# Three buffers instead of two for the filter and second-stage weight tiles of a Fourier transform, paid for out of the software DMA scratch

## The chip, the cores and the metric

The kernel runs on one core of a Trainium2 chip. The metric is the device time of one execution in microseconds (us). Engines are named as in the profile: PE is the matrix engine, PEld its weight loads, DVE the vector engine, ACT the scalar engine, POOL the general engine, SP the engine that here only issues transfers.

## What is computed

The input `x` has 8 batches of 3072 tokens with 256 channels. Three layers follow one another, all in float32:

```
Y   = rfft(x over tokens) * (filt_r + i filt_i);  y = irfft(Y)
k   = relu(xk @ w_k);  v = (k*k) @ w_v;  r = sigmoid(xr @ w_r);  x2 = r * v
h   = max(x2 @ w1, x2 @ w2, x2 @ w3);  out = h @ w_out
```

Here `xk` and `xr` are mixes of `y` with `y` shifted by one token. The hidden widths are 1024 (`w_k`, `w_v`) and 768 (`w1` to `w3`).

## The kernel before

**Precision.** Most products are made of three products of shortened operands: each operand is split into a high part (a copy by ACT) and the remainder (a subtraction by POOL or DVE), in `split` (lines 177 to 179), and `mm3` (line 155) issues the three matmuls. So nearly every matmul needs results of ACT and of POOL or DVE first.

**The transform.** The 3072-point transform of a batch is done in stages, each a matmul, with intermediate arrays `s1` and `s2` in DRAM. Batch 0 has its own code (`fft_first`, lines 423 to 562), before everything else. Batches 1 to 7 are done in `fft(b)` (lines 328 to 421), one batch ahead, in pieces that are threaded between the matmuls of the two dense layers by `drive` (line 108), by weights. Stage A has 16 steps (`a_load`, `a_mm`). Stages B and C have 12 steps for two groups of frequencies each:

- `b_load(s)` loads the weights of the step, tile `wbc` (512 KB, 4 KB in each of the 128 partitions; for batch 1 from the input through a software DMA that POOL issues, line 367, with a copy stored to DRAM by ACT, line 369; for later batches from that copy through SP, line 371), the filter, tile `filt` (512 KB, again 4 KB in each partition, line 373), and the data `xb` (line 375), which it splits into `xbh` (ACT) and `xbl` (POOL).
- `b_mm(s)` makes six matmuls with `wbc` (the profile calls the result `pb`), multiplies by the filter in place (DVE, lines 389 to 391, and POOL, line 392), and splits the product into `yh` and `yl` (line 395).
- `c_mm(s)` makes six matmuls with the other half of the same `wbc` tile (result `pc`) and stores the result to `s2`.

The order of the pieces is: `b_load(s)`, `b_mm(s-1)`, then `c_mm(s-2)`. A `wbc` tile is thus held from `b_load(s)` until `c_mm(s)`, two steps later; a `filt` tile from `b_load(s)` until `yl` has been made, one step later.

**Buffers.** Pool `fp` has two buffers for each tag. Tiles of one tag share these buffers:

```
f = fp.tile([NK, 2, 2, C], F32, tag="filt", name="filt")     # line 372; "wst" of piece(), lines 197, 199
w = fp.tile([NK, 4, 2, NK], F32R, tag="wbc", name="wbc")     # line 364; "wvs" 271, "hs" 292, "e1" 473
```

Tag `filt` also serves as the place into which the raw dense weights are loaded (`wst`, up to about 330 us); tag `wbc` also holds the split dense weights on their way to DRAM (`wvs`, `hs`) and one in three of the evacuated results of `fft_first` (`e1`). A transfer into a tile is issued only when the tile that used the buffer before has been read for the last time.

**The dense layers.** Tokens are handled in 64 chunks of 384. `kv` does the first layer for one chunk, `second` the second layer for a pair of chunks with seven products for a 2 by 2 block product. Their weights `w_v` and `w1` to `w3` are streamed anew for every chunk or pair through the pool `ws` (10 buffers, tile `ws`, line 265, up to 8 loads ahead, issued by SP). PE results in the second layer carry the names `pa`, `pb` and `pe` as well: `pb<-x,ws` is a matmul of the dense layer, `pb<-xbh,wbc` one of the transform.

**Order.** Every engine and every issuing queue works in order. Outside `fft_first` that order is laid down when the program is built, from a simulated timeline (`schedule_with_timeline_sim=True`, line 936), in which the order of the code is the priority. SP's order is written out by hand up to line 862.

**Scratch.** [...] POOL issues 17 transfers in all: one of `wa_s` (line 167), four of `wvs` (line 273), 12 of `wbc` (line 367).

Of the kernel before, what the change touches and what calls it, by code (L numbers as in the profile page):

```python
# [9 lines left out]
F32 = mybir.dt.float32  # L10
F32R = mybir.dt.float32r
I32 = mybir.dt.int32
# [11 lines left out]
NK = 2 * N2  # L24
# [70 lines left out]
def as_float(bits):  # L95
    return float(np.uint32(bits).view(np.float32))
# [29 lines left out]
def tile_spectral_moe(ctx: ExitStack, tc, x, filt, ones, wa, wa1, wi, wbc, wb1, wc1, filt1, filt0, mu, w_k, w_v, w_r, w1, w2, w3, w_out, out):  # L126
    nc = tc.nc
    B = x.shape[0]
    P = 128
    C = 256  # L130
# [13 lines left out]
    fp = ctx.enter_context(tc.tile_pool(name="fp", bufs=2))  # L144
# [7 lines left out]
    def mm(o, wgt, rhs, start, stop, more=False):  # L152
        nc.tensor.matmul(o, lhsT=wgt, rhs=rhs, start=start, stop=stop, skip_group_check=more)  # L153
# [23 lines left out]
    def split(hi, lo, src, lo_eng=None):  # L177
        nc.scalar.copy(hi, src)  # L178
        (lo_eng or nc.gpsimd).tensor_tensor(lo, src, hi.bitcast(F32), ALU.subtract)  # L179
# [4 lines left out]
    def piece(src, kt, t0, t1, c0, c1, parts):  # L184

        wide = src.dtype != F32
        if wide:
            src = src.bitcast(I32)
        v = src.rearrange("(t p) n -> p t n", p=P)
        a, c = t1 - t0, c1 - c0  # L190
        st = {}

        def load(stage=None):
            if stage is not None:
                st["t"] = stage.rearrange("p (a n) -> p a n", a=a)
            elif wide:
                st["t"] = fp.tile([P, a, 2 * c], I32, tag="filt", name="wst")
            else:
                st["t"] = fp.tile([P, a, c], F32, tag="filt", name="wst")
            k = 2 if wide else 1  # L200
            nc.sync.dma_start(st["t"], v[:, t0:t1, k * c0 : k * c1])

        def narrow(late=True):
            if not wide:
                st["r"] = st["t"]
                return
            w = st["t"].rearrange("p a (n k) -> p a n k", k=2)
            low, high = w[:, :, :, 0], w[:, :, :, 1]

            e = fp.tile([P, a, c], I32, tag="fo", name="we")  # L210
            ef = e.bitcast(F32)
            nc.scalar.activation(ef, high.bitcast(F32), AF.Abs)
            nc.vector.tensor_scalar(ef, ef, as_float(0x38000000), as_float(0x47EFFFFF), op0=ALU.max, op1=ALU.min)
            nc.vector.tensor_scalar(e, e, 3, 0x3FFFFFFF, op0=ALU.logical_shift_left, op1=ALU.bitwise_and)
            nc.vector.scalar_tensor_tensor(e, high, -0x40000000, e, ALU.bitwise_and, ALU.bitwise_or)
            m = fp.tile([P, a, c], I32, tag="fin", name="wm")
            mf = m.bitcast(F32)
            nc.vector.tensor_scalar(m, e, -0x800000, None, op0=ALU.bitwise_and)
            nc.vector.scalar_tensor_tensor(mf, low.bitcast(U32), 2.0**-52, mf, ALU.mult, ALU.mult)
            cnt[0] += 1  # L220
            r = fp.tile([P, a, c], F32, tag=("flo", "fhi")[cnt[0] % 2], name="wf")
            nc.gpsimd.tensor_tensor(r, ef, mf, ALU.add)
            st["r"] = r

        return load, narrow, lambda late=True: parts(st["r"], late)

    def to_parts(hi, lo, r, late):
        if late:
            nc.scalar.copy(hi, r)
        else:  # L230
            nc.vector.tensor_copy(hi, r)
        nc.gpsimd.tensor_tensor(lo, r, hi.bitcast(F32), ALU.subtract)
# [35 lines left out]

    def wv_job(q):
        def parts(r, late):  # L270
            t = fp.tile([P, 2, 2, C], F32R, tag="wbc", name="wvs")
            to_parts(t[:, :, 0], t[:, :, 1], r, late)
            nc.gpsimd.dma_start(wv_d[q], t.bitcast(F32))

        return piece(w_v, NF, 2 * q, 2 * q + 2, 0, C, parts)

    def wu_job(k):

        fq, j = divmod(k, 3)

        def parts(r, late):


            b11, b12, b21, b22 = (r[:, q, n * P : (n + 1) * P] for q in range(2) for n in range(2))
            sums = [[(0, b11)], [(0, b22), (1, b12), (0, b11)], [(0, b21)], [(0, b12), (1, b11)],
                    [(0, b22), (1, b12)], [(0, b22)], [(0, b12), (1, b11), (1, b22), (0, b21)]]
            for a, e in ((0, 4), (4, 7)):
                q = ps.tile([P, e - a, P], F32, tag="pm", name="ps")
                for n in range(a, e):
                    for at, (sign, of) in enumerate(sums[n]):  # L290
                        mm(q[:, n - a], eye[:, sign], of, n == a and at == 0, at == len(sums[n]) - 1, True)
                t = fp.tile([P, 4, 2, P], F32R, tag="wbc", name="hs")[:, : e - a]
                nc.scalar.copy(t[:, :, 0], q)
                nc.vector.tensor_tensor(t[:, :, 1], q, t[:, :, 0].bitcast(F32), ALU.subtract)
                nc.sync.dma_start(wu_d[k][:, a:e], t.bitcast(F32))

        return piece((w1, w2, w3)[j], 2, 0, 2, 2 * P * fq, 2 * P * (fq + 1), parts)
# [30 lines left out]
    def fft(b):  # L328
# [5 lines left out]
        st = {}  # L334
# [26 lines left out]
            pieces.append((0.65, pa))  # L361

        def b_load(s):
            w = fp.tile([NK, 4, 2, NK], F32R, tag="wbc", name="wbc")
            if b == 1:

                nc.gpsimd.dma_start(w, wbc[:, s])
                wbc_d[s] = dp.tile([NK, 4, 2, NK], F32, tag=f"wbcd{s}", name=f"wbcd{s}", bufs=1)
                nc.scalar.dma_start(wbc_d[s], w.bitcast(F32))
            else:  # L370
                nc.sync.dma_start(w.bitcast(F32), wbc_d[s])
            f = fp.tile([NK, 2, 2, C], F32, tag="filt", name="filt")
            nc.sync.dma_start(f, filt[:, s])
            t = fp.tile([NK, 2, C], F32, tag="fin", name="xb")
            nc.sync.dma_start(t, s1.rearrange("m r g c -> (m r) g c")[:, 2 * s : 2 * s + 2, :])
            hi = fp.tile([NK, 2, C], F32R, tag="fhi", name="xbh")
            lo = fp.tile([NK, 2, C], F32R, tag="flo", name="xbl")
            split(hi, lo, t)
            st["b", s] = w, f, hi, lo
# [27 lines left out]
        for s in range(NBS + 2):  # L407
            def pb(s=s):
                if s < NBS:
                    b_load(s)  # L410
                if 1 <= s <= NBS:
                    b_mm(s - 1)
            def pc(s=s):
                if s >= 2:
                    c_mm(s - 2)
            pieces.append((0.65, pb))
            if s == 0:

                pieces.append((6.0, lambda: None))
            pieces.append((0.65, pc))  # L420
        return pieces

    def fft_first(pp, jobs):
# [7 lines left out]
        p = ps.tile([P, 2, C], F32, tag="pm", name="pz")  # L431
# [7 lines left out]
        for s in range(NM // LX):  # L439
            t = pp.tile([NP, LX, C], F32, tag="big", name="x0", bufs=4)  # L440
# [29 lines left out]

        def evac(i, p, d, q=nc.sync):
            pool, tag = (fp, "wbc") if i % 3 == 2 else (pp, "fo1")
            o = pool.tile(list(p.shape), F32, tag=tag, name="e1", bufs=2 if pool is fp else 4)
            nc.scalar.copy(o, p)
            q.dma_start(d, o)

# [17 lines left out]
        for s in range(NM // 2):  # L494
            p = ps.tile([NQ, 2, C], F32, tag="pm", name="pa")
            mm(p, wa_f, xt[2 * s // LX][:, 2 * s % LX : 2 * s % LX + 2], True, True)
            evac(s, p, s1[2 * s : 2 * s + 2].rearrange("m r g c -> (r g) m c"))
            if s == 1:
                wb_load(0)
            if s == 4:  # L500
                nc.sync.dma_start(f0, filt0)
                f_load(0)
            if s == 6:
                wc_load(0)
                jobs[0][1](False)
                jobs[0][2](False)
# [17 lines left out]
        for s in range(NG // 2 + 2):  # L524
# [9 lines left out]
            if s < NG // 2:  # L534
                p = ps.tile([NK, 2, C], F32, tag="pm", name="pb")
# [3 lines left out]
                f = ft[s]  # L539
# [9 lines left out]
            if s >= 2:  # L549
                f, q = ft[s - 2], qs[s - 2]  # L550
                p = ps.tile([NK, 2, C], F32, tag="pm", name="pc")
                for k in range(2):
                    g = 2 * (s - 2) + k
                    mm(p[:, k], wt[g // LW][1][:, g % LW], f[:, k], True, False)
                    mm(p[:, k], wt[g // LW][2][:, g % LW], q[:, k], False, True)
                evac(s, p, s2.rearrange("m r g c -> (m r) g c")[:, 2 * s - 4 : 2 * s - 2, :], nc.scalar)
# [306 lines left out]
    for _ in range(8):  # L863

        p = ps.tile([P, NT], F32, tag="pm", name="pz")
# [102 lines left out]
```

## Time and profile before

| quantity | value |
|---|---|
| median of three runs | 3239.52 us (3239.22 to 3243.35) |
| profiled execution, first to last instruction (its span) | 3228.3 us |
| what lies around the span, against the median | 11.2 us |
| instructions | 55882 |
| PE busy | 3117.6 us, 97% of the span |
| DVE, ACT, POOL busy | 1774.2, 1918.9, 1865.8 us (55, 59, 58%) |
| bytes moved by transfers | 676 MB, 210 GB/s |

The profile is of one execution, taken by the hardware profiler. For the profiled execution itself nothing but its span is recorded; the 11.2 us is the median less that span. A wait is the time in which an engine sat idle ahead of an instruction, put down to what came last. [...]

### The profile page before, as it was taken

The page shows a single profiled execution, that of the slowest core. Times are in us where ns is not written, and L with a number is a line of the kernel's source. Part 1 is how long each engine was busy: PE and PEld are TensorE (multiplying, and loading weights), DVE is VectorE, ACT ScalarE, POOL GpSimd, SP SyncE. Part 2 cuts the span into 40 slices and gives each one's busy share as a digit, 9 for nine tenths or more (in the row PEclk, how much of TensorE's full clock was granted, in tenths as well). Part 3 has the DMA queues.
Part 4 walks back from the last instruction along what each step waited for, and adds up shares of the span by engine and source line. Part 5 has one row for each costly group of instructions (what it writes and reads, how often), then busy time and mean ns, then how long its engine had stood idle before and what let it go on. Part 6 is the DMA issues. An engine that isn't in the chain of part 4 may idle for free.

```text
span 3228.3 us, 55882 instructions
## 1 busy us (share of the span) xinstructions
PE 3117.6 (97%) x19256; PEld 3039.7 (94%) x19256; DVE 1774.2 (55%) x2882; ACT 1918.9 (59%) x4024; POOL 1865.8 (58%) x1619
## 2 busy tenths in 40 slices
PE   6799899999999999999999999999999999999998
PEld 4799889999999999999999999999999999999998
DVE  4865554556554565456545465445654456555554
ACT  5556556656566566656566556665656666555554
POOL 3545665557555675546756566565655567544443
PEclk8899999999999999999999999999999999999999
DMA  8767786657765676657766577655876657655553
GB/s 283 239 231 220 227 299 202 194 174 259 238 196 187 208 244 201 214 170 234 252 196 186 179 252 246 198 187 166 271 237 189 190 191 242 197 162 163 169 163 123
DMA packets 397783, 676.38 MB, mean 210 GB/s; under 512 B 41920, under 2 KB 153664, under 8 KB 396864
## 3 DMA queue, kind: packets, MB, share of 16 engines
q1 hardware_dynamic: 328336, 585.61, 57.1%
q10 hardware_dynamic: 66752, 78.75, 7.1%
q0 software_dynamic: 2416, 8.46, 0.9%
q8 instruction: 156, 2.56, 0.3%
q14 instruction: 123, 1.01, 0.1%
HBM read 580.51 MB, written 92.14 MB: 208 GB/s over the span
## 4 chain that ended last, share of the span: by engine, by line
PE 79%; DMA 8%; DVE 7%; issue 2%; ACT 2%; POOL 2%; SPq 0%; ACTq 0%; POOLq 0%; DVEq 0%
PE pb L153 18%; PE pk L153 13%; PE pv L153 13%; PE po L153 12%; PE pe L153 8%; PE pa L153 6%; PE pr L153 4%; PE py L153 3%; DMA wbc<-wbcd 3%; DMA ws<-wud 2%; PE pc L153 2%; DVE x L179 1%; DVE sc L665 1%; DMA wbc<-in_wbc 1%; POOL klo L179 1%
## 5 line engine op out<-in xcount | busy, mean ns | idle before, releaser
L153 PE MATMUL pb<-x,ws 128*128 128x384 f32 x3456 | 759.9, 339 | 15.6 <-DMA ws<-wud 12.4
L179 POOL TENSOR_TENSOR hh<-m,hh 128x384 fp32r<-128x384 f32 x384 | 398.7, 1046 | 557.4 <-ACT hh L178 446.1
L179 POOL TENSOR_TENSOR klo<-kr,khi 128x384 fp32r<-128x384 f32 x492 | 518.2, 1060 | 261.0 <-ACT khi L178 246.6
L153 PEld LDWEIGHTS pb<-x,ws 128*128 128x128 f32 x3456 | 600.7, 189 | 31.8 <-ACT u L701 7.1
L633 DVE SCALAR_TENSOR_TENSOR kr<-pk,kr 128x384 f32<-128x384 f32 x512 | 282.1, 554 | 496.3 <-ACT kr L632 495.0
L153 PE MATMUL po<-wo_hi,hh 128*128 128x256 f32 x2304 | 484.9, 283 | 5.9 <-ACT hh L178 3.3
L153 PE MATMUL pv<-khi,ws 128*128 128x384 f32 x2048 | 475.8, 338 | 7.3 <-ACT khi L178 7.2
L153 PEld LDWEIGHTS po<-wo_hi,hh 128*128 128x128 f32 x2304 | 391.3, 190 | 11.1 <-ACT hh L178 6.9
L153 PE MATMUL pe<-x,ws 128*128 128x384 f32 x1728 | 388.6, 337 | 0.0
L178 ACT CAST khi<-kr 128x384 fp32r<-128x384 f32 x512 | 260.6, 512 | 193.3 <-DVE kr L633 164.9
L153 PEld LDWEIGHTS pv<-khi,ws 128*128 128x128 f32 x2048 | 359.8, 188 | 12.7 <-ACT khi L178 11.9
L153 PE MATMUL pk<-xh,wk_hi 128*128 128x384 f32 x1024 | 341.4, 337 | 3.9 <-ACT xh L178 3.9
L153 PE MATMUL pk<-xl,wk_hi 128*128 128x384 f32 x1024 | 344.1, 336 | 0.2 <-DVE xl L179 0.2
L153 PE MATMUL pk<-xh,wk_lo 128*128 128x384 f32 x1024 | 344.0, 336 | 0.0
L632 ACT ACTIVATE kr<-pk 128x384 f32<-128x384 f32 x512 | 249.2, 489 | 117.1 <-PE pk L153 55.8
L153 PE MATMUL po<-wo_lo,hh 128*128 128x256 f32 x1152 | 317.5, 282 | 0.0
L748 DVE TENSOR_TENSOR m<-sc,m 128x384 f32<-128x384 f32 x384 | 311.5, 814 | 10.0
L153 PEld LDWEIGHTS pe<-x,ws 128*128 128x128 f32 x1728 | 298.8, 189 | 0.9 <-DVE sc L747 0.2
L153 PE MATMUL pv<-klo,ws 128*128 128x384 f32 x1024 | 293.0, 338 | 3.9 <-POOL klo L179 3.0
L179 POOL TENSOR_TENSOR xl<-xm,xh 128x768 fp32r<-128x768 f32 x126 | 233.6, 1869 | 101.3 <-ACT xh L178 101.3
L178 ACT CAST hh<-m 128x384 fp32r<-128x384 f32 x384 | 193.8, 515 | 147.9 <-DVE m L748 80.4
L701 ACT COPY v<-pb 128x384 f32<-128x384 f32 x288 | 138.5, 481 | 162.0 <-PE pb L153 156.5
(129 smaller groups left out, 6060.0 us busy)
## 6 DMA issues: line engine op xcount, KB each, us to landing
ws<-wud SPq DMA_DIRECT2D x864, 256.0 KB, 3.4
ws<-wvd SPq DMA_DIRECT2D x512, 256.0 KB, 3.2
filt<-in_filt SPq DMA_DIRECT2D x84, 512.0 KB, 5.1
ws<-wud SPq DMA_DIRECT2D x288, 128.0 KB, 3.5
wbc<-wbcd SPq DMA_DIRECT2D x72, 512.0 KB, 5.1
cin<-s SPq DMA_DIRECT2D x64, 384.0 KB, 4.2
out_dram<-osb ACTq DMA_DIRECT2D x192, 128.0 KB, 3.0
xb<-s SPq DMA_DIRECT2D x85, 256.0 KB, 3.5
```

Of the source, the lines that this page charges most:

```text
L153: nc.tensor.matmul(o, lhsT=wgt, rhs=rhs, start=start, stop=stop, skip_group_check=more)
L178: nc.scalar.copy(hi, src)
L179: (lo_eng or nc.gpsimd).tensor_tensor(lo, src, hi.bitcast(F32), ALU.subtract)
L632: nc.scalar.activation(r, p, AF.Relu)
L633: nc.vector.scalar_tensor_tensor(r, p, 0.0, r, ALU.max, ALU.mult)
L665: eng.tensor_tensor(t, a, b, ALU.subtract)
L701: nc.scalar.copy(st[to], st[of])
L748: nc.vector.tensor_tensor(m, c, m, ALU.max)
```

## The change

All tiles of tags `filt` and `wbc` ask for three buffers instead of two, which takes 4 KB more of each partition for each tag, 8 KB together. The program object is made with a scratch of 4096 bytes instead of 16384, which leaves 12 KB of each partition free. No instruction is added or taken out in the code, and no other tile is touched.

```diff
-                st["t"] = fp.tile([P, a, 2 * c], I32, tag="filt", name="wst")
+                st["t"] = fp.tile([P, a, 2 * c], I32, tag="filt", name="wst", bufs=3)
             else:
-                st["t"] = fp.tile([P, a, c], F32, tag="filt", name="wst")
+                st["t"] = fp.tile([P, a, c], F32, tag="filt", name="wst", bufs=3)
...
-            t = fp.tile([P, 2, 2, C], F32R, tag="wbc", name="wvs")
+            t = fp.tile([P, 2, 2, C], F32R, tag="wbc", name="wvs", bufs=3)
...
-                t = fp.tile([P, 4, 2, P], F32R, tag="wbc", name="hs")[:, : e - a]
+                t = fp.tile([P, 4, 2, P], F32R, tag="wbc", name="hs", bufs=3)[:, : e - a]
...
-            w = fp.tile([NK, 4, 2, NK], F32R, tag="wbc", name="wbc")
+            w = fp.tile([NK, 4, 2, NK], F32R, tag="wbc", name="wbc", bufs=3)
...
-            f = fp.tile([NK, 2, 2, C], F32, tag="filt", name="filt")
+            f = fp.tile([NK, 2, 2, C], F32, tag="filt", name="filt", bufs=3)
...
-            o = pool.tile(list(p.shape), F32, tag=tag, name="e1", bufs=2 if pool is fp else 4)
+            o = pool.tile(list(p.shape), F32, tag=tag, name="e1", bufs=3 if pool is fp else 4)
...
-    nc = _bacc.Bacc("TRN2", target_bir_lowering=False, num_devices=1)
+    nc = _bacc.Bacc("TRN2", target_bir_lowering=False, num_devices=1, dynamic_dma_scratch_size=4096)
```

## Rows read from the trace of the kernel before

**Rows 1.** The page, part 1: busy time, share of the span, instructions

```profile
PE 3117.6 (97%) x19256; PEld 3039.7 (94%) x19256; DVE 1774.2 (55%) x2882; ACT 1918.9 (59%) x4024; POOL 1865.8 (58%) x1619
```

**Rows 2.** Busy time by window: engines' busy us (count), PE clock, DMA share, GB/s

```profile
0.00:161.40 161.40, 119.17 (x549) 95.82 (x549) 104.78 (x161) 86.06 (x154) 73.98 (x62) 0.86 0.80 261
...
340.00:470.00 130.00, 113.90 (x698) 109.42 (x697) 73.37 (x115) 68.14 (x140) 90.81 (x81) 0.95 0.83 274
...
846.00:1068.00 222.00, 220.36 (x1373) 215.93 (x1373) 109.77 (x183) 140.25 (x299) 125.83 (x111) 1.00 0.61 190
1068.00:1233.00 165.00, 160.72 (x1010) 158.59 (x1010) 100.67 (x162) 96.62 (x202) 109.71 (x93) 0.99 0.74 241
...
2783.00:3147.30 364.30, 364.17 (x2299) 363.83 (x2298) 190.57 (x325) 210.20 (x454) 175.73 (x159) 1.00 0.52 164
```

**Rows 3.** Waits of PE: us in total, times, longest us

```profile
PE pb L153 <- DMA wbc<-wbcd: 20.9, 14, 2.8
PE pb L153 <- DMA ws<-wud: 12.4, 14, 2.9
...
PE py L153 <- ACT wr_hi L229: 10.6, 1, 10.6
...
PE pb L153 <- DMA wbc<-in_wbc: 8.4, 6, 2.3
```

**Rows 4.** Timeline of PE, one step: start us, us, instruction, idle before it

```profile
1199.27 0.28 PE L153 MATMUL pc<-yh,wbc 128*128 128x256 f32 x1
...
1201.88 1.20 PE L153 MATMUL pb<-x,ws 128*128 128x384 f32 x6
...
1206.38 0.35 PE L153 MATMUL pb<-xbh,wbc 128*128 128x256 f32 x1 [2.77 <-DMA wbc<-wbcd]
...
1207.36 3.08 PE L153 MATMUL pb<-x,ws 128*128 128x384 f32 x9
```

**Rows 5.** Timeline of SP, the same step and the next load of its kind

```profile
1200.17 0.32 SPq L371 DMA_DIRECT2D wbc<-wbcd  x1
...
1217.28 0.32 SPq L371 DMA_DIRECT2D wbc<-wbcd  x1
```

**Rows 6.** Tile wbc: its loads through POOL, and time from issue to landing

```profile
L367 POOL DMA_DIRECT2D wbc<-in_wbc x12: 545/580/585, 224.2 to 457.8; - x12
...
DMA to landing us min/median/max: 3.4/5.2/8.8
```

**Rows 7.** Timeline of POOL, the same step

```profile
1196.86 1.28 POOL L179 TENSOR_TENSOR xbl<-xb,xbh 128x512 fp32r<-128x512 f32 x1
```

**Rows 8.** Windows of 10 us after waits: columns as in rows 2

```profile
385.00:395.00 10.00, 6.48 (x25) 6.19 (x26) 2.38 (x4) 1.73 (x3) 5.91 (x6) 0.66 0.74 234
...
1203.00:1213.00 10.00, 7.24 (x35) 6.95 (x34) 5.16 (x9) 3.73 (x9) 2.58 (x2) 0.83 0.75 273
...
2753.00:2763.00 10.00, 7.90 (x39) 7.61 (x38) 5.29 (x9) 4.03 (x9) 2.86 (x3) 0.83 0.79 267
```

**Rows 9.** Waits of SP's queue: us in total, times, longest us

```profile
SPq L373 <- POOL yl L179: 133.0, 53, 4.7
...
SPq L201 <- DVE wm L219: 56.5, 14, 15.4
SPq L371 <- PE pc L153: 48.7, 56, 1.7
```

**Rows 10.** Timeline of SP in another step

```profile
2257.63 0.33 SPq L373 DMA_DIRECT2D filt<-in_filt  x1
2258.05 4.76 SPq L265 DMA_DIRECT2D ws<-wud  x5
```

**Rows 11.** Timeline of PE in that step

```profile
2264.24 1.28 PE L153 MATMUL pb<-x,ws 128*128 128x384 f32 x6 [1.08 <-DMA ws<-wud]
```

**Rows 12.** Transfers: software queue (packets, MB, share), POOL's loads of wbc

```profile
q0 software_dynamic: 2416, 8.46, 0.9%
...
wbc<-in_wbc POOLq DMA_DIRECT2D x12, 512.0 KB, 6.4
```

## The prediction

> **What bounds the kernel now.** I read the engines' shares first: PE is busy for 97% of the span, the other three for under 60% [rows 1]. So time can come only from PE's idle time, 110.7 us in all, and from PE's work at half clock. Next the windows, to see where that idle time lies [rows 2]. Up to 161 us PE idles 42.2 us (window less busy time). From 340 to 470 us, where stages B and C of batch 1 run, 16.1 us. Later the batches repeat: in 222 us without those stages 1.6 us is lost, in the 165 us with them 4.3 us. After the last transform, from 2783 us, 364 us pass with 0.1 us lost. So the transform's stages B and C cost PE something, and the dense layers alone nearly nothing. Third, who PE waits for [rows 3]: of the waits that recur, those for `wbc` lead, 20.9 us in 14 for the load through SP and 8.4 us in 6 for batch 1's load through POOL, 29.3 us together. Then 12.4 us for `ws`. The 10.6 us is a single wait at the start.
>
> Fourth, one step in order of time. `c_mm` starts at 1199.27, and its six matmuls free a `wbc` buffer [rows 4]; SP issues the next load at 1200.17 [rows 5]; a load lands after 3.4 to 8.8 us, 5.2 in the middle [rows 6]; `b_mm`, which needs it, starts at 1206.38 after 2.77 us of idle PE [rows 4]. The distance from `c_mm` to that `b_mm`, 7.1 us here, is about what issue and landing take (0.9 and 5.2 us), so a slower landing is a wait. The other operand was ready long before: `xbl` ended at 1198.14 [rows 7], 8.2 us ahead of `b_mm`. PE's waits name no `xbl` at all. The chain that ends last in these steps is buffer free, load, `b_mm`.
>
> **The change, part by part.**
>
> *Third buffer for `wbc`.* The load of step s no longer needs the buffer of step s-2 but that of s-3, freed one step earlier: loads are 17.11 us apart in the step shown (1200.17 to 1217.28 [rows 5]), and 13.7 us when 12 steps are spread over the 165 us window. Against a longest wait of 2.8 us [rows 3] that is ample, even with the slowest landing of 8.8 us [rows 6]. Removed: 20.9 + 8.4 = 29.3 us. SP's own waits for this buffer, 48.7 us in 56 [rows 9], end earlier too; they are off PE's path.
>
> *Half clock behind those waits.* After the wait of 2.77 us nine matmuls take 3.08 us, where six took 1.20 us before it [rows 4]; the clock in that window is 0.83 [rows 8], so 10 x 0.17 = 1.7 us is lost. Windows at 360, 1978, 2364 and 2753 us read 0.83 too, each behind a wait for `wbc` of over 2 us: five times 1.7 is 8.5 us. The window at 385 us reads 0.66, or 3.4 us lost, and holds a wait for `klo` beside the one for `wbc`; I count half, 1.7 us. Removed: 10.2 us; bounds 8.5 and 11.9.
>
> *Third buffer for `filt`.* SP waits 133.0 us in 53 times until `yl` has been made and the filter's buffer is free, up to 4.7 us [rows 9]. No engine waits for the filter's landing, so what this costs is what stands behind it on SP: `ws` loads. At 2257.63 the filter is issued, at 2258.05 the `ws` load behind it [rows 10], and PE waits 1.08 us for that one [rows 11]; a like case near 719 us costs 0.48 us. Of the 14 waits for `ws` over the span [rows 3] the others have no blocked filter ahead of them. Removed: 1.6 us; bounds 0 and the whole 12.4.
>
> *Tiles at the start (`wst`, `wvs`, `hs`, `e1`).* SP waits 56.5 us for a `wst` buffer [rows 9]. But PE's idle time up to 161 us comes from other things: the 10.6 us wait [rows 3] ends when batch 0's result has come back from DRAM. I take nothing. The third buffer moves 512 KB loads ahead of it or beside it, so the bounds are 3 us either way, an estimate from landings of 3.4 to 8.8 us for transfers of that size [rows 6], half the difference rounded up.
>
> *Smaller scratch.* The software queue carries 2416 packets in the whole run [rows 12], 151 for each of 16 engines, in 17 transfers. [...] The 12 loads are spread from 224.2 to 457.8 us [rows 6], so few are in flight at once: I take nothing. [...]
>
> Nothing else is added: no instruction, no byte moved. Sum: 29.3 + 10.2 + 1.6 = 41.1 us, or 3187.2 us of span; with the 11.2 us that lie between span and median, **3198.4 us**. What is late next is the rest of `ws` (10.8 us), and `khi`; both are there today.
>
> **The rivals.**
>
> *Moved by a part only.* SP's queue is in order, and the order comes from a simulated timeline. If the loads stay behind `ws` loads that wait for PE, they may move by about 1 us and not by a step. Then each of the 20 waits shrinks by up to 1 us: 17 us, and 5 us of half clock. 3239.5 - 22 is 3217 us. For it: SP is crowded. Against: today the load leaves 0.9 us after the start of `c_mm`, so the queue is not what holds it.
>
> *Nothing comes of it.* The third buffer is not used earlier, or what it gives is lost to waits elsewhere in the same stage: 3233 to 3246 us. Against: the dense layers alone run with 0.1 us lost in 364 [rows 2].
>
> *The order is redrawn, slower.* With `wbc` there early, the simulated timeline may put `b_mm` earlier in PE's order, right behind `xbl`. On the chip POOL may then be late, PE waits, and everything queued behind `b_mm` waits with it. Place: the 70 steps that reuse a buffer (10 in each of 7 batches). Price: today's mean wait, 29.3 / 20 = 1.47 us, each time is 103 us, plus half clock at today's rate (10.2 / 20 = 0.5 us each), 36 us; against 41 saved that gives 3337 us. It decides from 0.6 us a step (41.1 / 70). Against: `b_mm` would have to move up by 8.2 us first [rows 7], and steps are spaced by weights, not by readiness.
>
> *Loads in the way.* Landing times are up to 8.8 us where the engines' share is 0.74 [rows 2, 6]. Two more prefetched tiles could delay `ws` loads: if its waits doubled, 12.4 us come back, 3211 us. The rate stays one load per step, so I count it into the range. [...]
>
> **How the numbers follow.** The forecast (3186 to 3212, loads in the way included) 0.68; moved by a part (to 3233) 0.15; nothing 0.08; slower 0.09. Low end: the remaining 10.8 us of `ws` waits go as well, and the 1.7 us of clock, 3186. High end: the partial case whole, 3232. That leaves out nothing, slower, and a little at the edges, 2 in 10. A measurement of this kernel can tell about 0.2%, 6.5 us, from no change. Faster by more than that takes the first two cases, 0.83; same 0.08; slower 0.09.
>
> **What would show it.** Right: no wait of PE for `wbc` over 0.5 us; the load issued about one step before; windows with these stages at 1.00 clock and below 3 us idle; SP's waits for `yl` and `pc` mostly gone; POOL's 12 loads with no longer waits. Wrong: PE waiting for `xbl` or `xbh` ahead of `b_mm` (redrawn); `wbc` waits of half the size (by a part); `ws` waits above 20 us (in the way).

## The result and the profile after

The changed kernel takes 3199.02 us (median of six runs, 3198.04 to 3202.12). The kernel before took 3225.64 to 3243.35 us in six runs, median 3234.41: the three from ahead of the prediction lie at 3239.22 or above, the three new ones at 3229.61 or below. The ratio is 0.9893, with a 95% interval of 0.9877 to 0.9910: faster by 1.1%. The forecast was 3198.4 us, faster, so value and direction came out; that the value came out to within 1 us was luck, as the section on the prediction shows: two terms behind it were off by 9 us each and cancelled. One further run of the kernel before, beside the first four experiments, took 6840.34 us; its cause is not known, and it stands in no ratio here.

First the page, part 1, of the kernel after, beside [rows 1].

```profile
span 3196.4 us, 55749 instructions
...
PE 3105.7 (97%) x19256; PEld 3031.7 (95%) x19256; DVE 1784.9 (56%) x2882; ACT 1913.8 (60%) x4024; POOL 1864.1 (58%) x1619
```

The span fell by 31.9 us (3228.3 to 3196.4): PE's idle time by 20.0 us (110.7 to 90.7, span less busy) and PE's busy time by 11.9 us, with the same 19256 matmuls. Next the waits of PE after, us in total, times, longest; beside [rows 3].

```profile
PE pb L153 <- DMA ws<-wud: 16.9, 16, 2.3
PE py L153 <- DMA eye<-in_ones: 12.2, 1, 12.2
...
PE pc L153 <- DVE filt L391: 3.8, 1, 3.8
...
PE pa L153 <- DMA ws<-wud: 1.4, 3, 0.8
```

There is no row for `wbc` left: 29.3 us in 20 waits have gone to nothing. The waits for `ws` (both results) rose from 13.0 to 18.3 us and now lead. The other 4.0 us of the balance (29.3 - 5.3 - 20.0) are the net of small waits in PE's redrawn order. The largest that are new: 5.0 us for the filter product of batch 1 (3.8 of them in the row above), 2.7 us for `co`, 2.4 us more for `v` and 2.3 us more for `xh`; others became shorter.

The step itself, on PE and on SP, beside [rows 4, 5]:

```profile
1177.42 0.28 PE L153 MATMUL pc<-yh,wbc 128*128 128x256 f32 x1
...
1183.33 0.28 PE L153 MATMUL pb<-xbh,wbc 128*128 128x256 f32 x1
...
1190.46 0.28 PE L153 MATMUL pc<-yh,wbc 128*128 128x256 f32 x1
...
1197.76 0.28 PE L153 MATMUL pb<-xbh,wbc 128*128 128x256 f32 x1
```

```profile
1178.95 0.38 SPq L371 DMA_DIRECT2D wbc<-wbcd  x1
...
1191.36 0.32 SPq L371 DMA_DIRECT2D wbc<-wbcd  x1
```

The load still leaves 1.5 and 0.9 us after the start of a `c_mm`. But the `b_mm` that starts 5.9 us after the first of these `c_mm` no longer needs it: matched by their order, the load of 1178.95 is for the `b_mm` of 1197.76. In the nine steps of a batch that reuse one of its three buffers, over batches 2 to 7, a load has landed 10.4 us or more before its `b_mm` (middle 14.2 us); in the same 54 steps it was 0.1 us or more before the change (middle 0.3).

To keep the start out of it, I compare from the first `b_mm` of batch 2 to that of batch 7, five whole batches and 11880 matmuls. The window view, columns as in [rows 2], of the kernel before:

```profile
687.30:2619.60 1932.30, 1901.66 (x11881) 1867.59 (x11880) 1052.57 (x1720) 1182.08 (x2491) 1176.65 (x1016) 1.00 0.66 212
```

and of the kernel after, with the window of batch 1 ahead of it:

```profile
340.00:470.00 130.00, 124.05 (x792) 120.36 (x792) 83.79 (x130) 78.82 (x165) 99.69 (x89) 0.99 0.87 292
...
678.80:2592.30 1913.50, 1894.48 (x11882) 1863.02 (x11882) 1060.79 (x1720) 1177.41 (x2491) 1178.55 (x1016) 1.00 0.68 214
```

Five batches take 18.8 us less; PE's idle time in them falls from 30.6 to 19.0 us. Of the rest of the 31.9 us, batch 1 (from its own first `b_mm` to that of batch 2) gives 13.5 and what follows the window 4.6, while the stretch ahead of batch 1's first `b_mm` is 5.0 us longer. In batch 1's window, of equal length, idle time falls from 16.1 to 6.0 us and PE gets 792 matmuls done instead of 698.

### The profile page after: what moved, and what is told of

Read it like the earlier page. It is cut to its first block, busy times and chain, and to the rows that moved or that the text cites. A ratio compares the mean times of both kernels' runs of the same rounds, so it can differ in the third digit from the quotient of the medians.

```text
span 3196.4 us, 55749 instructions
## 1 busy us (share of the span) xinstructions
PE 3105.7 (97%) x19256; PEld 3031.7 (95%) x19256; DVE 1784.9 (56%) x2882; ACT 1913.8 (60%) x4024; POOL 1864.1 (58%) x1619
## 4 chain that ended last, share of the span: by engine, by line
PE 84%; DMA 6%; DVE 5%; issue 2%; ACT 2%; POOL 1%; ACTq 0%; SPq 0%; POOLq 0%; DVEq 0%
PE pb L153 19%; PE pk L153 14%; PE pv L153 14%; PE po L153 12%; PE pe L153 9%; PE pa L153 7%; PE pr L153 4%; PE py L153 3%; DMA ws<-wud 3%; PE pc L153 2%; DVE xm L607 1%; DMA xb<-s 1%; PE ps L153 1%; DVE sc L665 1%; DVE m L748 1%
## 5 line engine op out<-in xcount | busy, mean ns | idle before, releaser
L607 DVE SCALAR_TENSOR_TENSOR xm<-yt,nmu_s,xm 128x384 f32<-128x384 f32 x256 | 180.1, 748 | 145.4 <-ACT xm L606 145.4
```

What stands on the lines that cost most here:

```text
L607: nc.vector.scalar_tensor_tensor(v[:, h], yt[:, h, :, :MC], nmu_s[:, w, h : h + 1], v[:, h], ALU.mult, ALU.add)
```

## The experiments

All ratios are to the kernel before, run beside it on the same chip, with 95% intervals. Theory A: what the change removes is PE's wait for a `wbc` load that can't start before a buffer is free.

**One tag at a time.** The changed kernel with `bufs=3` taken back at `filt` and `wst`:

```diff
-            f = fp.tile([NK, 2, 2, C], F32, tag="filt", name="filt", bufs=3)
+            f = fp.tile([NK, 2, 2, C], F32, tag="filt", name="filt")
```

> Third buffer for tag wbc alone, two for filt, scratch 4096. Theory A (the wait of b_mm for the wbc load is what the change removes): nearly all of the gain, 0.988 to 0.992 of before; no wait of PE for wbc. Rival B (the filter's buffer counts, because a blocked SP delays the ws stream): at most a third of the gain, 0.996 or above. PE's ws waits as in the changed kernel (15 to 20 us) by both.

Measured 0.9891 (0.9876 to 0.9906), the whole gain, as the change's 0.9893. PE's waits have no row for `wbc`, and 18.3 us for `ws`, most of it in

```profile
PE pb L153 <- DMA ws<-wud: 17.0, 16, 2.1
```

Then the reverse, three buffers for `filt`, two for all tiles of `wbc`:

```diff
...
-            w = fp.tile([NK, 4, 2, NK], F32R, tag="wbc", name="wbc", bufs=3)
+            w = fp.tile([NK, 4, 2, NK], F32R, tag="wbc", name="wbc")
```

> Third buffer for tag filt alone, two for wbc, scratch 4096. Theory A: within 0.2% of before (0.998 to 1.002), the 20 waits for wbc still there with 25 to 33 us, SP's waits for yl mostly gone. Rival B: 0.992 to 0.996.

Measured 1.0006 (0.9995 to 1.0017): nothing. PE's waits and SP's own, of this kernel, in two views:

```profile
PE pb L153 <- DMA wbc<-wbcd: 19.4, 16, 3.0
...
PE pb L153 <- DMA wbc<-in_wbc: 9.8, 5, 3.0
```

```profile
SPq L373 <- POOL yl L179: 131.4, 56, 4.5
```

The filter's third buffer does not even shorten SP's wait for `yl`, 133.0 us in [rows 9]: SP's order now asks for the filter one step sooner (30.9 us ahead of its use in the middle, 17.2 before) and waits there for the buffer of one step further back. The load leaves 0.03 us, in the middle, after `yl` of three steps back, where it was two. So this half of the expectation was wrong, and the half on the time right.

**The scratch alone.**

```diff
-    nc = _bacc.Bacc("TRN2", target_bir_lowering=False, num_devices=1)
+    nc = _bacc.Bacc("TRN2", target_bir_lowering=False, num_devices=1, dynamic_dma_scratch_size=4096)
```

> Before with a scratch of 4096 bytes and no third buffer; the order of every engine is the same as before, only addresses move. Theory A: no difference, 0.998 to 1.002, POOL's loads of wbc land as fast (6 to 7 us) and take 0.55 to 0.6 us to issue. Rival C (the smaller scratch makes POOL wait): over 1.002, with issue times of some us in batch 1. It also shows how much the time of one and the same order wanders from run to run.

Measured 1.0003 (0.9993 to 1.0013). POOL's 12 loads of `wbc`, ns min, middle and max to issue:

```profile
L367 POOL DMA_DIRECT2D wbc<-in_wbc x12: 542/578/582, 226.6 to 463.2; - x12
```

This is what [rows 6] show with 16 KB, and the loads land after 5.9 us in the middle (6.4 with 16 KB), so the small scratch costs nothing here. With one and the same order, 12 runs lie between 3225.10 and 3239.10 us.

**More distance with two buffers.** Before, with the pieces' weights changed:

```diff
-            pieces.append((0.65, pb))
+            pieces.append((0.35, pb))
...
-            pieces.append((0.65, pc))
+            pieces.append((0.95, pc))
```

> Before with two buffers and the old scratch; only the weights of the pieces change, 0.35 for b_load/b_mm and 0.95 for c_mm in place of 0.65 each, so that c_mm is followed by the b_mm whose load it frees some 10 us later and not 7. Theory A: the load lands in time though there is no third buffer; the waits for wbc fall from 29 to under 8 us and the time to 0.989 to 0.994. Rival D (the gain comes from the redrawn order elsewhere or needs the third buffer): 0.997 or above. If the shorter way from b_mm to c_mm is too short for yl, PE waits for yl instead and the time comes out above before.

Measured 0.9961 (0.9946 to 0.9976): between the theories. From `c_mm` to the `b_mm` two steps later it is now 8.6 us in the middle of 60 steps of batches 2 to 7, against 7.0 before: the order moved by 1.6 us and not by 3. Waits for `wbc` fell from 29.3 to 15.4 us, and those for `klo` rose from 3.0 to 8.7 us:

```profile
PE pb L153 <- DMA wbc<-wbcd: 10.6, 11, 2.2
...
PE pv L153 <- POOL klo L179: 8.7, 9, 1.2
PE pb L153 <- DMA wbc<-in_wbc: 4.8, 5, 2.4
```

The waits fall with distance, as theory A has it, but the weights only partly set that distance. In the kernel before, too, distance tells where PE waits. PE's order repeats from batch 2 on (the same 2376 matmuls in the same order in each of the five batches from 687.3 to 2619.6 us), and 12 of PE's 14 waits for `wbc` in batches 2 to 7 lie at three of the twelve steps (3, 10 and 11, counted from 0), where 25, 21 and 35 matmuls stand between a `c_mm` and the `b_mm` that needs its buffer; at the others it is 31 to 49.

**The needed half first.** Before, with two transfers per load, so that `b_mm` waits for one half:

```diff
-                nc.sync.dma_start(w.bitcast(F32), wbc_d[s])
+                nc.sync.dma_start(w[:, :2].bitcast(F32), wbc_d[s][:, :2])
+                nc.sync.dma_start(w[:, 2:].bitcast(F32), wbc_d[s][:, 2:])
```

> Before with two buffers and the old scratch, but batches 2 to 7 load wbc in two transfers of 256 KB, the half that b_mm needs first. Theory A1 (only the chip's landing counts: a half lands some 1.8 us sooner, as other 256 KB loads do with 3.4 us against 5.2): the waits of batches 2 to 7 fall from 19 to 21 us to under 8, time 0.993 to 0.997. Rival A2 (the place of b_mm in PE's order follows the landing that the simulated timeline gives, so a quicker load only moves b_mm up): the waits stay, 12 us or more, b_mm follows c_mm after some 5 us in place of 7, and the time is 0.997 to 1.003.

Measured 0.9946 (0.9934 to 0.9959), in the range of theory A1. The first half lands after 4.2 us in the middle (5.1 before), and PE's waits read

```profile
PE pb L153 <- DMA ws<-wud: 22.0, 21, 3.9
...
PE pb L153 <- DMA wbc<-in_wbc: 8.5, 5, 2.4
...
PE pb L153 <- DMA wbc<-wbcd: 0.6, 2, 0.3
```

The waits of batches 2 to 7 are gone with two buffers; batch 1's stay, since its loads were left whole; those for `ws` grew by 9 us, here too. Rival A2 falls, but it has a true part. From `c_mm` to `b_mm` it is 6.8 us in the middle, yet PE's order was redrawn: at steps 3, 10 and 11 there are now 31, 39 and 39 matmuls between the two, and at step 8 `b_mm` moved up, from 31 to 19. The order alone would not have done away with the waits: in 26 of the 60 steps the second half landed only after `b_mm` had started, up to 2.4 us after it and 17.5 us in all, and there a whole load would have held PE up. As the second half also leaves 0.37 us after the first, that is an upper bound; with 0.4 us taken off each time, 8.7 us stay. So by this estimate the early half is worth some 9 to 18 of the 20 us of waits that went, and the new order the rest.

**The waits for `ws`.** They lead after the change, so the 4 KB left over went to two more `ws` buffers:

```diff
-    AHEAD = 8
+    AHEAD = 10
...
-    ws = ctx.enter_context(tc.tile_pool(name="ws", bufs=10))
+    ws = ctx.enter_context(tc.tile_pool(name="ws", bufs=12))
```

> The changed kernel with 12 buffers for ws in place of 10 (in the 4 KB that the change left free) and 10 loads ahead in place of 8. If the waits for ws (18 us now, the largest that recur) come from too little lead: they fall below 8 us and the time to 0.993 to 0.997 of the changed kernel, 0.982 to 0.986 of before. If they come from SP being held by other waits: within 0.2% of the changed kernel, 0.987 to 0.991 of before.

Measured 0.9819 (0.9806 to 0.9832), 3174.01 us: faster than both kernels. The same with `AHEAD = 8`:

> The changed kernel with 12 buffers for ws but still 8 loads ahead. If the lead in the code's order counts: as the changed kernel, 0.987 to 0.991 of before, ws waits 15 to 20 us. If a buffer that comes free too late is what delays a ws load: as with 10 ahead.

Measured 0.9823 (0.9810 to 0.9836). With 12 buffers a lead of 8 does as well as one of 10, so it is the buffer that counts. The waits for `ws` are down to 1.6 us, and the window of five batches reads

```profile
PE pb L153 <- DMA ws<-wud: 1.6, 2, 1.4
```

```profile
676.20:2570.60 1894.40, 1889.34 (x11883) 1863.92 (x11882) 1060.67 (x1720) 1176.04 (x2491) 1178.30 (x1016) 1.00 0.68 216
```

19.1 us less than with the change alone, 5.1 us idle left. One more buffer only, beside a third one for `wbc`:

> Third buffer for wbc alone and 11 buffers for ws. If one more buffer covers the late ws loads: 0.981 to 0.984, ws waits below 3 us, as with 12. If each buffer gives its share: 0.985 to 0.988, ws waits of 6 to 12 us.

Measured 0.9851 (0.9832 to 0.9871), waits for `ws` 4.6 us: the time says that each buffer gives its share, the waits lie between the two branches. And the filter's room used for `ws` too, 14 buffers and 12 ahead:

> Third buffer for wbc alone, and the rest of the freed room for ws: 14 buffers and 12 loads ahead. By theory A the filter's third buffer is worth nothing, so at least as fast as with 12 and 10 ahead: 0.980 to 0.986 of before if lead counts, 0.987 to 0.991 if not.

Measured 0.9825 (0.9812 to 0.9837): no better than 12, and no worse for two filter buffers instead of three. PE's waits have no row for `ws` left.

**Are the two costs separate?** Before, two buffers for `wbc`, 12 for `ws`, small scratch:

> Before with two buffers for wbc and filt, 12 for ws and a scratch of 4096. If the waits for ws and those for wbc are separate costs: the ws waits (13 us before) fall below 3, the wbc waits stay at 17 to 24 us, the time is 0.992 to 0.996. If the waits for ws were mostly made by the third buffer of wbc: 0.997 or above.

Measured 0.9955 (0.9938 to 0.9972). The waits for `wbc` stay, those for `ws` go:

```profile
PE pb L153 <- DMA wbc<-wbcd: 18.2, 14, 2.9
...
PE pb L153 <- DMA wbc<-in_wbc: 7.2, 5, 2.9
...
PE pb L153 <- DMA ws<-wud: 1.1, 1, 1.1
```

So the two costs are separate, but they do not quite add up: 0.45% here and 1.07% for the change make 1.5%, and both together gave 1.8%. That fits with the 5.3 us of `ws` waits which the change alone brings in and which the 12 buffers take away as well. Then 12 buffers for `ws` and the load in halves, as above:

> Two buffers for wbc, its load in two halves, 12 buffers for ws, scratch 4096. If the third wbc buffer does nothing but take the wait for the load away, halves do the same for batches 2 to 7 and only batch 1's waits (8 us and some half clock) remain: 0.982 to 0.987. If the third buffer gives more than that: 0.988 or above.

Measured 0.9875 (0.9855 to 0.9895), between the two ranges. Where the halves act, in batches 2 to 7, they equal the third buffer:

```profile
693.10:2588.00 1894.90, 1890.67 (x11881) 1863.86 (x11881) 1052.57 (x1720) 1178.30 (x2491) 1180.87 (x1016) 1.00 0.68 216
```

1894.90 us for five batches, against 1894.40 with three buffers. The rest of the difference lies ahead of that window, which starts at 693.1 us instead of 676.2, and all of it in batch 1: from its first `b_mm` to that of batch 2 it takes 347.1 us, against 329.8. So last, batch 1's loads in halves too, on POOL (scratch 12288):

```diff
-                nc.gpsimd.dma_start(w, wbc[:, s])
+                nc.gpsimd.dma_start(w[:, :2], wbc[:, s, :2])
+                nc.gpsimd.dma_start(w[:, 2:], wbc[:, s, 2:])
```

> As with halves and 12 buffers for ws, but batch 1's loads through POOL come in halves as well; two buffers for wbc, scratch 12288. If the 15 us that still lay between halves and the third buffer are batch 1's late loads: waits for its wbc load fall from 8 us below 2, time 0.982 to 0.985 of before. If batch 1 needs the buffer itself (its store to DRAM also holds the buffer, and twice as many loads go through POOL): 0.986 to 0.990, with waits for the load still at 5 us or more.

Measured 0.9880 (0.9860 to 0.9900). It did not help. Waits of PE from 340 to 485 us, where the first row was 7.9 us with whole loads in batch 1:

```profile
PE pb L153 <- DMA wbc<-in_wbc: 15.8, 5, 4.8
...
PE pv L153 <- DMA wbcd<-wbc: 1.0, 1, 1.0
```

So in batch 1 halves do not stand in for the third buffer. The store, which the expectation names as a reason, is not it: in all ten steps that reuse a buffer, the store that read this buffer had landed 6.9 us or more ahead of the end of the `c_mm` that freed it. The trace shows two other things. PE's order was redrawn: at six of the ten steps fewer matmuls stand between `c_mm` and `b_mm` than with whole loads (6 in place of 19 at the tightest), while the first half lands only 1.2 us sooner (5.1 us in the middle, 6.3 whole). And POOL issued two of the loads 3.0 and 4.1 us after that `c_mm` had ended, ahead of the two longest waits (4.8 and 4.1 us). How much each of these costs, and whether the doubled issues count, was not told apart.

## Why the prediction was right, and where it was wrong

*Third buffer for `wbc`: right.* 29.3 us were forecast to go, and all went. Taking this buffer alone gives the whole result, and the reason holds when it is reached in another way: waiting for half of the load, which lands 0.9 us sooner, does away with the waits of batches 2 to 7 as well, with some help of a new order. One reading was off: the slowest landing, 8.8 us, is that of a load at 476 us, near which the engines' share is 0.88 (470 to 490 us), and not of the stage with 0.74.

*Half clock: right, a little small.* 10.2 us forecast; PE's busy time fell by 11.9 us. In the records the granted clock is either 1.0 or 0.5, and a window's figure is the mean over it: before, it reads 1.00 from 1200 to 1206 us, ahead of and in the wait of 2.77 us, and 0.50 from 1207 to 1210 us, behind it. These records say the same as the busy time: 39.6 us were lost to the lower level over the span before, 27.8 us after. All spells that the prediction counted are gone, the one at 385 us whole, of which I had counted half. In the window of five batches there were three, each behind a wait for `wbc`, and there is none after. Two spells are new, each behind another wait; one is this, after the 3.8 us wait for the filter product of batch 1, where the clock column reads 0.83:

```profile
406.00:416.00 10.00, 6.35 (x30) 6.18 (x31) 4.91 (x9) 6.03 (x14) 6.30 (x7) 0.83 0.65 207
```

*Third buffer for `filt`: wrong.* I counted 1.6 us of `ws` waits off, as I took SP's wait for `yl` to hold up the `ws` loads. Alone it gives 1.0006. SP's wait stays (133.0 to 131.4 us alone, 106.4 in the changed kernel); what delays a `ws` load is the `ws` buffer, as 12 buffers with the old lead show. In SP's waits after the change the two rows read

```profile
SPq L373 <- POOL yl L179: 106.4, 55, 6.6
...
SPq L371 <- PE pc L153: 29.4, 63, 0.9
```

The sign "SP's waits for `yl` and `pc` mostly gone" was wrong for the same reason.

*The sum: 9 us too large.* What was not in it are waits that came in with PE's new order: `ws` 5.3 us up instead of 1.6 down, and 4.0 us of others. "Its waits doubled" was in the range as loads in the way. The runs speak against that reason: the same bytes are moved, and a `ws` load lands after 3.4 us in the middle before and after. The waits for `ws` also rise, to 22.2 us, with two `wbc` buffers and halves. What these kernels share is a new order, much the same in all, and a PE that `wbc` no longer holds up while `ws` loads land. Which of the two is the reason was not tested.

*The anchor: 9 us too high.* I took 11.2 us as what lies between span and device time. In each profiled execution since, it is 1.8 us (3198.21 and 3196.4 here). So the one profiled before took about 3230.1 us, and the 11.2 us was mostly the scatter of its runs. Against its own time the sum says 3189.0 us (3230.1 - 41.1); measured 3198.2. The two errors of 9 us cancel in 3198.4: the mechanism was right, the last digits of the value were luck.

*Start and scratch: right.* No gain from either. No run shows how the transfers use the scratch; what is measured is POOL's time to issue its 12 loads, 542 to 582 ns in the kernel with the small scratch alone and 545 to 585 ns before. That the room is there the experiments show: with 4096 bytes a kernel ran with 12 KB more of tiles in a partition than before (three buffers for `wbc`, 14 for `ws`), with 12288 bytes one with 4 KB more (12 for `ws`). The first `b_mm` of batch 1 came at 346.1 us against 341.2, but at 344.5 with the unchanged order too, so most of that is scatter.

*The rivals.* "Moved by a part" falls: the load gains a whole step. "Redrawn, slower" had a true part, PE's order is much changed (at 4406 of 19256 places stands a matmul of another kind), but PE waits for `xbl` nowhere. With a third buffer for `filt` alone 205 places change, so it is `wbc` that redraws it. My argument that weights and not readiness space the steps was too strong: the experiment with shifted weights moved `b_mm` by half of what the weights asked.

## What to carry to other kernels

Where a load waits for its buffer and the consumer waits for the load, look at what the consumer waits and at the clock it loses behind these waits: here one more buffer took away 29.3 us of waits and 11.9 us of busy time, and 9.3 us came back as other waits. Look also at how long each buffer is held and by whom, since loading first the half that is needed first did the same here in batches 2 to 7, though not in batch 1. Give the room to the tile for whose landing the bottleneck engine waits, not to the one for which the issuing queue waits: SP waited 133 us for filter buffers, and that was worth nothing, while 2 KB buffers for `ws` were worth 0.2 to 0.4% each. Then read the waits again: here the next ones, 18.3 us for `ws`, came from the same shortage in the neighbouring pool, and 12 buffers brought them down to 1.6 us.

## What the runs showed that was not expected

Kernels with two `wbc` buffers scatter more from run to run. The kernel before spans 17.7 us over six runs, and 14.0 us over 12 with the small scratch; the changed kernel spans 4.1 us over six. All six kernels with a third `wbc` buffer span 4.1 to 8.1 us, the seven changed kernels with two 8.9 to 14.2 us, in 4 to 12 runs each. That landing times, 3.4 to 8.8 us [rows 6], reach the end of the run only where PE waits for them would explain part of it. It was not tested by itself, and the kernel with halves and 12 `ws` buffers speaks against it as the whole reason: PE waits there for `wbc` almost only in batch 1, 7.9 us, and its four runs still span 14.2 us.
